# The last two chunks of an attention and mixer kernel: order of ScalarE's copies, step size of the weight sums, and the last pair's banks

## The chip, the cores and the metric

One core of a Trainium2 chip runs the whole program. The metric is the device time of one execution in microseconds. Before the change three runs took 777.46, 777.44 and 774.66 us, median 777.44.

## The reference

The first half is an attention over 32 memory slots per head: weights `a` are a softmax of `phi` over the sequence, they pool keys and values (`k_m`, `v_m`), and each query attends to the pooled keys. Its output, as `x` of 8 x 576 rows and 512 channels, goes through a mixer:

```python
xt = x.transpose(0, 2, 1)
h = np.maximum(xt @ w_tok1, 0.0) @ w_tok2
u = x + h.transpose(0, 2, 1)
h2 = np.maximum(u @ w_ch1, 0.0) @ w_ch2
return (u + h2).astype(np.float32)
```

The change lies in `u + relu(u @ w_ch1) @ w_ch2`, with 1536 hidden channels, for the last 1024 of the 4608 rows.

## The kernel before, in words

All products are made from pairs of parts: a number is split into a high part of fewer bits and the rest (`hh` and `hl`, `c2h` and `c2l` and so on), and three matmuls (high by high, high by low, low by high) stand for one product. The 4608 rows are cut into nine chunks of 512. Chunks 0 to 6 are of no interest here but for their end. Chunks 7 and 8 are of class `Sevens` (L325): there the products with `w_ch1` and with `w_ch2` are both done by a scheme of seven products of half blocks in place of eight (names 11, 22, T1, T3, T2, 21, T4), so that sums and differences of blocks have to be made on VectorE, and split again.

One call of `seven(c, p)` (L2163) handles the pair `p` of hidden blocks, of six, in chunk `c`. TensorE makes the seven first products (six matmuls of 256 columns each) of this pair, with weights in small units that `load_unit` (L539) brings from DRAM, three units ahead. In between, as filling, `mix` hands out the 42 matmuls of the second products of the pair before (`seconds`, L364), which add into seven PSUM banks `m11` to `mT4` (`open_banks`, L339); `shares` says how many come at each of four steps. In the first call, (7,0), the filling is what is left of chunk 6.

The first products use one bank only, `one`, with two halves `a` and `b`. So each step is: two products, a copy of the bank by ScalarE (L2255, L2267, L2281, and of one half L2295), the filling, and then what VectorE and ScalarE make of the copies: adds of the results `r11`, `r12`, `c22`, their ReLU (L2239), the differences T1 to T4, and the split of each into a high part (ScalarE, L124 and L2232) and a low part (VectorE, L127 and L2236). The next products may not write the bank before it is copied. The product T4 of a call is left over to the beginning of the next one.

Every engine takes its instructions in the order of the program text. Besides the pair's own work, `events_at` puts work from other places into the steps, from a table of due times (L1955 to L2059); a call has times `24c + 4p` to that plus 3.5, so (7,0) is 168 to 171.5. Among these are the inputs of chunk 8 (`high`, `low` and the four differences at L276 to L287) and `Tops` (L418): for each of the six pairs of `w_ch2` blocks it makes the sums that the second products need: `words` (high plus low part, 1024 columns, L426), `sum` (four of 256 columns, L465), `high` (L474), `low` (L478). The four due times of a pair are half a unit apart, and the pairs start at 157, 160, 163, 173, 166 and 177. Their results go to rooms that other tiles have left; pairs 0 to 3 have rooms that let one instruction split all four sums, pairs 4 and 5 take four each.

When the last second products of a chunk are done (chunk 7's in (8,0), chunk 8's in (8,5)), `drain` (L379) adds the banks into the output tile `u`: eleven VectorE adds of 512 columns and one ScalarE copy, at the end of the step in which each bank is complete. The last pair of chunk 8 is not done by seven products: its first products give `hid`, the hidden values themselves, and after all of the filling the end (L2333 to L2341) multiplies them with `w_ch2` into five fresh banks, adds each to `u` (L200) and stores it.

Of the kernel before, what the change touches and what calls it, by code (L numbers as in the profile page):

```python
# [20 lines left out]
P = 128  # L21
# [7 lines left out]
def kernel(  # L29
# [295 lines left out]
    class Sevens(Quarters):  # L325
# [38 lines left out]
        def seconds(s, p):  # L364

            for name in ("11", "22", "T1", "T3", "T2", "21", "T4"):
                lh, ll = s.left(name, p)
                h, l = s.right(name)
                for a in range(2):
                    for x, (l_, r) in enumerate(((lh, h), (lh, l), (ll, h))):  # L370
                        first, last = not (a or x or p), a == 1 and x == 2
                        yield 1, name if last else None, lambda name=name, a=a, l_=l_, r=r, first=first: (
                            nc.tensor.matmul(  # L373
                                s.banks[name][:, a], l_[:, a * P : a * P + P], r,
                                start=first, stop=False, skip_group_check=True,
                            )
                        )

        def drain(s, name):  # L379
            V, m = f32(s.rooms2["V"]), s.banks  # L380

            def add(to, x):
                o = s.quarter(int(to[0]) - 1, int(to[1]) - 1) if to != "V" else V
                nc.vector.tensor_tensor(out=o, in0=x, in1=o, op=ALU.add)

            if name == "11":
                nc.scalar.copy(out=V, in_=m["11"])
                add("11", m["11"])
            elif name == "22":
                add("12", m["22"])  # L390
            elif name == "T1":
                add("12", m["T1"])
                add("22", m["T1"])
            elif name == "T2":
                add("V", m["T2"])
                add("12", V)
                add("V", m["T3"])
                add("21", V)
                add("22", V)
            elif name == "21":  # L400
                add("11", m["21"])
            elif name == "T4":
                add("21", m["T4"])

# [13 lines left out]
    class Tops:  # L418
# [5 lines left out]
        def words(s):  # L424
            s.w = sb.tile([P, 2, DM], F32, tag="big", name=f"cw{s.p}", bufs=1)
            nc.vector.tensor_tensor(out=s.w, in0=f32(c2h[s.p]), in1=f32(c2l[s.p]), op=ALU.add)  # L426

        def rooms(s):
            def quad(pool, tag):
                return pool.tile([P, 4, HW], F32R, tag=tag, name=f"top{tag}", bufs=1)  # L430

            if s.p in (0, 3):
                tag = ("kv", "rest")[s.p // 3]
                t = sb.tile([P, 2, 4, HW], F32R, tag=tag, name=f"top{tag}", bufs=1)
                s.merged = [(t[:, 0], t[:, 1])]
            elif s.p < 3:
                s.merged = [tuple(quad(wp, f"w{s.p}{x}") for x in "hl")]
            elif s.p == 4:
# [12 lines left out]
            if s.merged:  # L451
                ((h, l),) = s.merged
                s.pieces = [(h[:, o], l[:, o]) for o in range(4)]
            Sevens.tops[s.p] = dict(zip(("T2", "T3", "22", "T1"), s.pieces))

        def sum(s):
            s.rooms()
            a11, a21, a12, a22 = s.w4 = [s.w[:, j, HW * i : HW * i + HW] for j in range(2) for i in range(2)]
            for to, x, y, op in (
# [4 lines left out]
            ):  # L464
                nc.vector.tensor_tensor(out=to, in0=x, in1=y, op=op)  # L465

        def parts(s):
            if s.merged:
                return [(*s.merged[0], s.w.rearrange("p j (i n) -> p (j i) n", i=2))]
            return [(h, l, w) for (h, l), w in zip(s.pieces, s.w4)]  # L470

        def high(s):
            for h, l, w in s.parts():
                nc.scalar.copy(out=h, in_=w)  # L474

        def low(s):
            for h, l, w in s.parts():
                nc.vector.tensor_tensor(out=l, in0=w, in1=f32(h), op=ALU.subtract)  # L478

# [58 lines left out]

    def load_unit(n):  # L539
        if n >= 2 * NF * (CHUNKS - WIN):  # L540
# [4 lines left out]
        m = 512 if j == 3 else 1024  # L545
        nc.scalar.dma_start(out=f32(t)[:, :m], in_=sums[p].to[:, j, :m])

# [1506 lines left out]
    for n in range(AHEAD):  # L2054
        at(2 * NF * WIN - 4 + n, load_unit, n, k=1)
    for p, h in enumerate((157, 160, 163, 173, 166, 177)):
        top = Tops(p)
        for x, fn in enumerate((top.words, top.sum, top.high, top.low)):
            at(h + x / 2, fn, k=1)  # L2059

# [99 lines left out]

    one, left = [], []

    def seven(c, p):  # L2163
# [9 lines left out]
        T = {**Sevens.T, "T4": C[:, 3]}  # L2173
        todo, final, done, unit = [], None, [], []
        if begin:
            for x, f in before:
                for a in range(NKK):
                    def fn(x=x, f=f, a=a):
                        x.ch2(f, [a])
                        if f == x.end - 1:  # L2180
                            x.add(a)
                    todo.append((6, None, fn))
        else:
            x, f = before
            if not ch.banks:
                ch.open_banks()
            todo += x.seconds(f)
            final = x if f == x.end // 2 - 1 else None
        shares = (12, 12, 12, 12) if begin else (10, 10, 9, 6, 7) if end else (12, 11, 11, 8)

        def mix(x):
            n = shares[x] if x < len(shares) else 0
            while n > 0 and todo:
                cost, name, fn = todo.pop(0)
                fn()
                n -= cost
                if name and final:
                    done.append(name)

        def drains():  # L2200
            for name in done:
                final.drain(name)
            done.clear()
# [74 lines left out]
        events_at(1, 1.5)  # L2278
        product(5, "22", b, False)
        product(2, "T2", a, False)  # L2280
        nc.scalar.copy(out=st3, in_=X)  # L2281
        mix(2)
        add(r12, st3[:, 0], st3[:, 1])
        if end:
            relu_high(eh[:, t1], r12)
            relu_low(eh[:, t1], el[:, t1], r12)
        else:
            relu(r12)
            sub(T["T1"], r12, r11)
            T_high("T1")  # L2290
            T_low("T1")
        drains()
        events_at(2, 2.5)
        product(4, "T3", a, False)
        nc.scalar.copy(out=c22, in_=a)  # L2295
        mix(3)
        add(c22, c22, st2[:, 1])
        if end:
            relu_high(oh[:, t1], c22)
            relu_low(oh[:, t1], ol[:, t1], c22)  # L2300
        else:
            high("22", c22)
            sub(T["T3"], c22, r12, True)
            T_high("T3")
            low("22", c22)
            add(T["T2"], T["T3"], r11)
            T_high("T2")
            T_low("T3")
            T_low("T2")
        drains()  # L2310
        events_at(3, 3.5)

        def rest():
            ch.first(a, units[n + 3][:, 0], "T4", False)
            load_unit(n + 3 + AHEAD + 1)

        if end:
            rest()
            mix(4)
            relu_high(oh[:, t0], a)  # L2320
            relu_low(oh[:, t0], ol[:, t0], a)
            drains()
        else:
            left.append(rest)
        assert not todo, todo
        return ch, p
# [99 lines left out]
```

## Time and profile before

| what | us |
|---|---|
| median of three runs | 777.44 |
| lowest and highest | 774.66, 777.46 |
| the profiled execution | 779.87 |
| its span | 778.1 |
| TensorE, matmul busy | 752.4 |
| VectorE busy | 526.1 |
| ScalarE busy | 377.6 |

The span is what the hardware profiler saw of one execution; the 1.8 us beside it lie around it. Busy time is not a limit by itself: a stage is bound by whatever the last of its waits is for. Engines are PE (matmuls on TensorE), PEld (its weight loads), DVE (VectorE), ACT (ScalarE), SP (SyncE). PEclk is the granted TensorE clock as a share of 2.4 GHz. The profile writes tile names without their numbers: `whole` is the tile that holds the copies of the first and the fourth step, `rst` those of the second and third, `m` and `mT` the seven banks, `cw` the sums of weights, `top...` the rooms for their splits, `unit` the first weights, `end` the banks of the last pair.

### The profile page before, as it was taken

How to read it: one execution, taken by the hardware profiler on the slowest of the kernel's cores; microseconds unless marked ns; L12 is line 12 of the kernel's file. 1: busy time of each engine (PE TensorE's matmuls, PEld its weight loads, DVE VectorE, ACT ScalarE, POOL GpSimd, SP SyncE). 2: the span in 40 equal slices, each digit the busy share in tenths (PEclk: the TensorE clock that was granted, in tenths of full speed). 3: DMA queues.
4: the chain of work that ended last, by engine and by line, in shares of the span. 5: the costliest groups of instructions: out<-in, count | busy, mean ns of one | idle time of the engine just before them, and what ended most of it. 6: DMA issues, size and time to landing. Idle time of an engine off the chain costs nothing.

```text
span 778.1 us, 13954 instructions
## 1 busy us (share of the span) xinstructions
PE 752.4 (97%) x5369; PEld 663.7 (85%) x5369; DVE 526.1 (68%) x1025; ACT 377.6 (49%) x841; POOL 83.5 (11%) x79
## 2 busy tenths in 40 slices
PE   9999999999999999999999999999999997998996
PEld 8787888888877888898988898989899887997996
DVE  4989863788486758655865486748555876677566
ACT  5899772333233335453635353536353544563561
POOL 2204323011220230000000000000010000000000
PEclk9999999999999999999999999999999998999999
DMA  9955623574618249694869386847574563554651
GB/s 367 381 207 169 216 92 96 143 258 129 217 32 281 50 156 290 198 299 133 273 202 274 117 255 231 238 158 206 195 206 113 171 200 112 162 164 152 212 166 54
DMA packets 90449, 147.38 MB, mean 189 GB/s; under 512 B 41488, under 2 KB 60304, under 8 KB 86160
## 3 DMA queue, kind: packets, MB, share of 16 engines
q1 hardware_dynamic: 68032, 79.63, 31.4%
q10 hardware_dynamic: 22352, 66.87, 27.7%
q8 instruction: 42, 0.69, 0.4%
q14 instruction: 23, 0.19, 0.1%
HBM read 121.57 MB, written 24.90 MB: 188 GB/s over the span
## 4 chain that ended last, share of the span: by engine, by line
PE 75%; DVE 12%; DMA 5%; ACT 4%; issue 2%; POOL 1%; SPq 0%; ACTq 0%; DVEq 0%; POOLq 0%
PE acc L182 24%; PE cp L159 9%; PE qa L320 8%; PE u L904 7%; PE one L416 6%; PE qb L320 6%; PE Ap L864 2%; PE mT L373 2%; PE m L373 2%; PE sp L720 1%; DMA kv<-in_kv_dram 1%; PE Rp L883 1%; DMA kb<-keys 1%; PE sp L621 1%; DMA unit<-sums 1%
## 5 line engine op out<-in xcount | busy, mean ns | idle before, releaser
L182 PE MATMUL acc<-qhh,c 128*128 128x512 f32 x256 | 99.4, 395 | 0.0
L182 PE MATMUL acc<-hh,c 128*128 128x512 f32 x288 | 96.7, 395 | 0.0
L320 PEld LDWEIGHTS qa<-xT,unit 128*128 128x128 f32 x432 | 61.1, 188 | 6.6 <-ACT whole L2105 0.5
L320 PEld LDWEIGHTS qb<-x,unit 128*128 128x128 f32 x432 | 61.2, 188 | 6.3
L182 PEld LDWEIGHTS acc<-hh,c 128*128 128x128 f32 x288 | 54.1, 188 | 14.4 <-issue 3.1
L320 PE MATMUL qa<-xT,unit 128*128 128x256 f32 x432 | 63.0, 281 | 0.1
L320 PE MATMUL qb<-x,unit 128*128 128x256 f32 x432 | 62.9, 281 | 0.0
L182 PE MATMUL acc<-hl,c 128*128 128x512 f32 x144 | 56.2, 390 | 0.0
L182 PEld LDWEIGHTS acc<-qhh,c 128*128 128x128 f32 x256 | 48.2, 188 | 9.1 <-issue 3.3
L182 PE MATMUL acc<-qal,c 128*128 128x512 f32 x192 | 54.6, 394 | 0.0
L2108 DVE TENSOR_TENSOR whole<-whole 128x256 f32<-128x256 f32 x48 | 20.7, 431 | 45.9 <-ACT whole L2105 45.9
L182 PE MATMUL acc<-qhl,c 128*128 128x512 f32 x128 | 50.9, 398 | 0.7 <-DVE qhl L127 0.7
L159 PE MATMUL cp<-uh,c1h 128*128 128x512 f32 x144 | 51.5, 398 | 0.0
L159 PE MATMUL cp<-ul,c1h 128*128 128x512 f32 x144 | 50.3, 390 | 0.0
L159 PE MATMUL cp<-uh,c1l 128*128 128x512 f32 x144 | 50.3, 390 | 0.0
L2105 ACT COPY whole<-qa 128x256 f32<-128x256 f32 x72 | 26.7, 371 | 47.8 <-PE qa L320 44.9
L127 DVE SCALAR_TENSOR_TENSOR hl<-cp,hh 128x512 fp32r<-128x512 f32 x36 | 24.7, 686 | 34.3 <-ACT hh L124 34.2
L416 PE MATMUL one<-x,unit 128*128 128x256 f32 x288 | 43.9, 298 | 1.7 <-ACT whole L2255 1.5
L416 PEld LDWEIGHTS one<-x,unit 128*128 128x128 f32 x288 | 40.0, 205 | 3.0 <-ACT whole L2255 2.1
L416 PE MATMUL one<-xT,unit 128*128 128x256 f32 x216 | 34.4, 297 | 7.9 <-ACT whole L2295 7.6
L416 PEld LDWEIGHTS one<-xT,unit 128*128 128x128 f32 x216 | 29.5, 198 | 10.0 <-ACT whole L2295 8.9
L2105 ACT COPY whole<-qb 128x256 f32<-128x256 f32 x48 | 17.7, 369 | 35.6 <-PE qb L320 35.5
(337 smaller groups left out, 1809.4 us busy)
## 6 DMA issues: line engine op xcount, KB each, us to landing
unit<-sums ACTq DMA_DIRECT2D x108, 512.0 KB, 3.9
kv<-in_kv_dram SPq DMA_DIRECT2D x12, 1280.0 KB, 8.3
rawc<-in_w_ch_dram SPq DMA_DIRECT2D x12, 1024.0 KB, 7.0
q<-in_q_dram SPq DMA_DIRECT2D x16, 576.0 KB, 6.0
unit<-sums ACTq DMA_DIRECT2D x36, 256.0 KB, 3.3
sums<-sums SPq DMA_DIRECT2D x12, 512.0 KB, 5.9
phi<-in_phi_dram SPq DMA_DIRECT2D x16, 320.0 KB, 5.5
out_dram<-u SPq DMA_DIRECT2D x5, 1024.0 KB, 5.0
```

The costliest lines, as they stand in the source:

```text
L127: nc.vector.scalar_tensor_tensor(out=l, in0=ps, scalar=0.0, in1=f32(h), op0=ALU.max, op1=ALU.subtract)
L159: nc.tensor.matmul(ps, l[:, a, w], r[:, a], start=n == 0, stop=n == len(mm) - 1)
L182: nc.tensor.matmul(ps, l_[f // 2][:, f % 2, a * P : (a + 1) * P], r[:, w], start=f == start and x == 0, stop=f == end - 1 and x == 2,)
L320: nc.tensor.matmul(ps[:, :HW], l, r, start=first and n == 0, stop=n == len(mm) - 1, skip_group_check=not first,)
L373: nc.tensor.matmul(s.banks[name][:, a], l_[:, a * P : a * P + P], r, start=first, stop=False, skip_group_check=True,)
L416: nc.tensor.matmul(ps, l, r, start=start and n == 0, stop=False, skip_group_check=True)
L621: nc.tensor.matmul(s.kvp[32 * i : 32 * i + 32, : 2 * D], s.pt[:, i, j, :], s.kv[:, :, j, i, :], start=j == 0, stop=j == NC - 1,)
L720: nc.tensor.matmul(s.sp[hf][m, :HALF], s.kb[w, m], s.qT[w, i], start=True, stop=True)
L864: nc.tensor.matmul(ps[:, :TT], a, w, start=x == 0, stop=x == len(mm) - 1)
L904: nc.tensor.matmul(ps[:, :HALF], a, r, start=x == 0, stop=x == len(mm) - 1)
L2105: nc.scalar.copy(out=to, in_=ps[:, :HW])
L2108: nc.vector.tensor_tensor(out=to, in0=x, in1=y, op=ALU.add)
```

## The change

1. Splits move. The differences T1, T3 and T2 are still made in the last step of a call, but their splits and that of `c22` now come in the next call: 22, T1 and T3 behind the copy of its first step, T2 behind the second, together with 21 and T4. The add of `r11` stays in the second step, its ReLU and split go to the third, behind the copy there; the add of `r12` stays in the third, its ReLU goes to the fourth.
2. The filling becomes one list, `stream`, that runs on over the calls, with shares 11, 11, 11, 9; in (7,1) they are 6, 11, 11, 8, so that six matmuls more are always left over from there on.
3. The adds of the banks become single entries of a list, `drains`, of which each step takes two or three, into the following call if need be.
4. `load_unit` in these calls issues from SP and no longer from ScalarE's queue.
5. `Tops` becomes one sequence of small steps, half a unit of time apart: `words` in two halves, four sums, then the copies, then the differences; splits of the whole become two of half the size. Pair 3 now takes rooms with four splits, pair 5 those with two. They start at 156, 161, 166, 171, 178 and 185.
6. The last pair: in place of fresh banks for 128 channels by 512 rows, the last pair's products go straight on top of three of the seven banks (22, 21 and T4), each the quarter that the bank belongs to, and of one free bank, with 12 matmuls of 256 columns each; the order is by which half of `hid` is ready first. These three banks are no longer drained by themselves.

The core of the diff:

```diff
+                return lambda: nc.vector.tensor_tensor(out=o, in0=x, in1=o, op=ALU.add)
+
+            return {
+                "11": [lambda: nc.scalar.copy(out=V, in_=m["11"]), add("11", m["11"])],
+                "22": [add("12", m["22"])],
+                "T1": [add("12", m["T1"]), add("22", m["T1"])],
+                "T3": [],
+                "T2": [add("V", m["T2"]), add("12", V), add("V", m["T3"]), add("22", V), add("21", V)],
+                "21": [add("11", m["21"])],
+                "T4": [add("21", m["T4"])],
+            }[name]
+
+        def direct(s, i, t, fs, ps, start=False):
+
+            for a in range(2):
+                for n, f in enumerate(fs):
+                    h, l = s.hid[f]
+                    for x, (l_, r) in enumerate(((c2h, h), (c2h, l), (c2l, h))):
+                        nc.tensor.matmul(
+                            ps[:, a],
+                            l_[f // 2][:, f % 2, (2 * i + a) * P : (2 * i + a + 1) * P],
+                            r[:, t * HW : (t + 1) * HW],
+                            start=start and not (a or n or x), stop=False, skip_group_check=True,
+                        )
...
-            nc.vector.tensor_tensor(out=s.w, in0=f32(c2h[s.p]), in1=f32(c2l[s.p]), op=ALU.add)
+            for j in range(2):
+                yield lambda j=j: nc.vector.tensor_tensor(
+                    out=s.w[:, j], in0=f32(c2h[s.p][:, j]), in1=f32(c2l[s.p][:, j]), op=ALU.add
+                )
...
+        def steps(s):
+
+            yield from s.words()
             s.rooms()
+            a11, a21, a12, a22 = w = [s.w[:, j, HW * i : HW * i + HW] for j in range(2) for i in range(2)]
             for to, x, y, op in (
                 (a22, a21, a22, ALU.add),
                 (a21, a11, a21, ALU.subtract),
                 (a11, a22, a11, ALU.subtract),
                 (a12, a12, a11, ALU.subtract),
             ):
+                yield lambda to=to, x=x, y=y, op=op: nc.vector.tensor_tensor(out=to, in0=x, in1=y, op=op)
+            parts = [(h, l, x) for (h, l), x in zip(s.pieces, w)]
             if s.merged:
+                parts = [
+                    (h, l, s.w[:, j].rearrange("p (i n) -> p i n", i=2)) for j, (h, l) in enumerate(s.merged)
+                ]
+            for h, l, x in parts:
+                yield lambda h=h, x=x: nc.scalar.copy(out=h, in_=x)
+            for h, l, x in parts:
+                yield lambda h=h, l=l, x=x: nc.vector.tensor_tensor(out=l, in0=x, in1=f32(h), op=ALU.subtract)
...
-    for p, h in enumerate((157, 160, 163, 173, 166, 177)):
-        top = Tops(p)
-        for x, fn in enumerate((top.words, top.sum, top.high, top.low)):
-            at(h + x / 2, fn, k=1)
+    for p, h in enumerate((156, 161, 166, 171, 178, 185)):
+        top = Tops(p).steps()
+        for x in range(14 if p in (3, 4) else 10):
+            at(h + x / 2, lambda top=top: next(top)(), k=1)
...
+            for name, fn in x.seconds(f):
+                stream.append((1, fn))
+                if name and f == x.end // 2 - 1 and not (x is ch and name in ("22", "21", "T4")):
+                    stream.append((0, lambda name=name, x=x: drains.extend(x.drain(name))))
-        shares = (12, 12, 12, 12) if begin else (10, 10, 9, 6, 7) if end else (12, 11, 11, 8)
-
-        def mix(x):
-            n = shares[x] if x < len(shares) else 0
...
-                load_unit(n + k // 2 + AHEAD + 1)
+                load_unit(n + k // 2 + AHEAD + 1, nc.sync)
...
-        mix(0)
+        mix(shares[0])
         if not begin:
+            high("22", c22)
+            T_high("T1")
+            T_high("T3")
+            low("22", c22)
+            T_low("T1")
+            T_low("T3")
             sub(T["T4"], st1[:, 0], T["T2"], True)
-            high("21", st1[:, 0])
-            T_high("T4")
-            low("21", st1[:, 0])
-            T_low("T4")
-        drains()
+        drain(3)
         events_at(0, 0.5)
         product(3, "T1", b, True)
         product(0, "11", a, False)
         nc.scalar.copy(out=st2, in_=X)
-        mix(1)
+        mix(shares[1])
+        if not begin:
+            T_high("T2")
+            high("21", st1[:, 0])
+            T_high("T4")
+            T_low("T2")
+            low("21", st1[:, 0])
+            T_low("T4")
         add(r11, st2[:, 0], st1[:, 1])
+        drain(2)
+        events_at(1, 1.5)
+        product(5, "22", b, False)
+        product(2, "T2", a, False)
+        nc.scalar.copy(out=st3, in_=X)
+        mix(shares[2])
         if end:
             relu_high(eh[:, t0], r11)
             relu_low(eh[:, t0], el[:, t0], r11)
...
             relu(r11)
             high("11", r11)
             low("11", r11)
-        drains()
-        events_at(1, 1.5)
-        product(5, "22", b, False)
-        product(2, "T2", a, False)
-        nc.scalar.copy(out=st3, in_=X)
-        mix(2)
         add(r12, st3[:, 0], st3[:, 1])
+        drain(2)
+        events_at(2, 2.5)
+        product(4, "T3", a, False)
+        nc.scalar.copy(out=c22, in_=a)
+        mix(shares[3])
+        add(c22, c22, st2[:, 1])
         if end:
             relu_high(eh[:, t1], r12)
             relu_low(eh[:, t1], el[:, t1], r12)
+            relu_high(oh[:, t1], c22)
+            relu_low(oh[:, t1], ol[:, t1], c22)
         else:
             relu(r12)
             sub(T["T1"], r12, r11)
-            T_high("T1")
-            T_low("T1")
-        drains()
-        events_at(2, 2.5)
-        product(4, "T3", a, False)
-        nc.scalar.copy(out=c22, in_=a)
-        mix(3)
-        add(c22, c22, st2[:, 1])
-        if end:
-            relu_high(oh[:, t1], c22)
-            relu_low(oh[:, t1], ol[:, t1], c22)
-        else:
-            high("22", c22)
             sub(T["T3"], c22, r12, True)
-            T_high("T3")
-            low("22", c22)
             add(T["T2"], T["T3"], r11)
-            T_high("T2")
-            T_low("T3")
-            T_low("T2")
-        drains()
+        drain(3)
         events_at(3, 3.5)
 
...
-    banks = [(pat, "at", 2)] * 2 + [(pacc, f"acc{a}", 1) for a in range(3)]
-    whole, halves = slice(0, CW), [slice(0, CW // 2), slice(CW // 2, CW)]
-    pieces = [(a, whole) for a in range(NKK - 1)] + [(NKK - 1, w) for w in halves]
-    for x, ((a, w), (pool, tag, n)) in enumerate(zip(pieces, banks)):
-        ps = pool.tile([P, CW], F32, tag=tag, name=f"end{x}", bufs=n)[:, : w.stop - w.start]
-        last.second(ps, a, range(last.end, NF), last.end, NF, w)
-        last.add(a, w, ps)
-        last.store(w, slice(a, a + 1), (nc.scalar, nc.sync)[x % 2])
+    free = pat.tile([P, 2, HW], F32, tag="at", name="free", bufs=2)
+    banks = {"12": last.banks["22"], "22": free, "11": last.banks["21"], "21": last.banks["T4"]}
+    for x, (name, ps) in enumerate(banks.items()):
+        i, t = int(name[0]) - 1, int(name[1]) - 1
+        last.direct(i, t, range(last.end, NF), ps, name == "22")
+        for fn in drains[: 2 - x // 2]:
+            fn()
+        del drains[: 2 - x // 2]
+        for a in range(2) if x == 3 else (slice(0, 2),):
+            o = last.quarter(i, t)[:, a]
+            nc.vector.tensor_tensor(out=o, in0=ps[:, a], in1=o, op=ALU.add)
+            (nc.scalar, nc.sync)[(x + (a == 1)) % 2].dma_start(
+                out=out[last.c, :, 2 * i : 2 * i + 2, t * HW : (t + 1) * HW][:, a], in_=o
+            )
+    assert not drains, drains
```

## Rows read from the trace of the kernel before

**Rows 1.** Page: busy time by engine; DMA issues, us to landing

```profile
PE 752.4 (97%) x5369; PEld 663.7 (85%) x5369; DVE 526.1 (68%) x1025; ACT 377.6 (49%) x841; POOL 83.5 (11%) x79
...
unit<-sums ACTq DMA_DIRECT2D x108, 512.0 KB, 3.9
```

**Rows 2.** Stretches of one call: length, busy us of each engine, clock, DMA

```profile
core 0: us, PE busy (x) PEld busy (x) DVE busy (x) ACT busy (x) POOL busy (x), PEclk, DMA share, GB/s
...
620.15:632.12 11.97, 10.47 (x62) 8.55 (x60) 9.62 (x21) 5.93 (x15) 0.00 (x0) 1.00 0.43 145
632.12:646.49 14.37, 11.13 (x84) 10.31 (x84) 10.34 (x23) 6.65 (x14) 0.00 (x0) 0.98 0.64 211
646.49:663.00 16.51, 13.28 (x84) 12.87 (x85) 11.06 (x25) 7.99 (x19) 0.00 (x0) 0.81 0.36 113
663.00:674.62 11.62, 11.62 (x85) 11.59 (x85) 7.10 (x18) 5.82 (x13) 0.00 (x0) 0.86 0.45 146
684.78:695.74 10.96, 10.58 (x87) 10.18 (x85) 7.58 (x19) 6.82 (x15) 0.00 (x0) 1.00 0.56 167
695.74:708.24 12.50, 10.83 (x85) 10.22 (x85) 10.31 (x24) 7.19 (x16) 0.00 (x0) 1.00 0.49 150
708.24:723.00 14.76, 12.35 (x85) 11.70 (x85) 9.98 (x23) 5.78 (x13) 0.00 (x0) 0.88 0.59 196
...
743.32:753.49 10.17, 10.17 (x87) 10.14 (x85) 5.70 (x16) 5.79 (x13) 0.00 (x0) 1.00 0.61 182
```

**Rows 3.** Waits of PE, 560 to 778.1: total us, times, longest

```profile
PE one L416 <- ACT whole L2295: 7.6, 5, 3.1
PE end L182 <- DVE hid L127: 2.4, 1, 2.4
```

**Rows 4.** Time line around one long wait: start, length, what, idle before

```profile
641.74 1.81 DVE L465 TENSOR_TENSOR cw<-cw 128x256 f32<-128x256 f32 x4
643.91 0.42 ACT L2239 ACTIVATE rst<-rst 128x256 f32<-128x256 f32 x1 [2.40 <-DVE rst L2229]
645.13 1.04 ACT L474 CAST toprest<-cw 128x1024 fp32r<-128x1024 f32 x1
646.08 0.36 ACT L2295 COPY whole<-one 128x256 f32<-128x256 f32 x1
646.49 1.65 PE L416 MATMUL one<-xT,unit 128*128 128x256 f32 x6 [2.61 <-ACT whole L2295]
```

**Rows 5.** Stretches after that wait, columns as in rows 2

```profile
646.50:648.00 1.50, 1.50 (x7) 1.50 (x8) 1.47 (x3) 0.20 (x1) 0.00 (x0) 0.50 0.66 265
653.00:654.00 1.00, 1.00 (x11) 1.00 (x10) 0.00 (x0) 0.20 (x1) 0.00 (x0) 1.00 0.33 131
```

**Rows 6.** Time line of the end of the last call and the tail

```profile
767.65 0.42 DVE L127 SCALAR_TENSOR_TENSOR hid<-one,hid 128x256 fp32r<-128x256 f32 x1
768.12 6.50 PE L182 MATMUL end<-hid,c 128*128 128x512 f32 x26 [2.41 <-DVE hid L127]
774.66 0.42 DVE L200 TENSOR_TENSOR u<-end,u 128x256 f32<-128x256 f32 x1 [0.29 <-PE end L182]
```

**Rows 7.** Time line of a call without excess

```profile
734.04 0.42 DVE L127 SCALAR_TENSOR_TENSOR r<-whole,r 128x256 fp32r<-128x256 f32 x1
734.38 0.42 DVE L2229 TENSOR_TENSOR sT<-sT,rst 128x256 f32<-128x256 f32 x1
735.26 0.59 ACT L2255 COPY whole<-one 128x512 f32<-128x512 f32 x1
736.34 0.41 ACT L2232 CAST rT<-whole 128x256 fp32r<-128x256 f32 x1
736.35 0.33 ACTq L546 DMA_DIRECT2D unit<-sums  x1
```

**Rows 8.** Groups of instructions, 640 to 778.1: busy us, mean ns of one

```profile
L426 DVE TENSOR_TENSOR cw<-c 128x1024 f32<-128x1024 f32 x2 | 2.4, 1218 | 0.0
L384 DVE TENSOR_TENSOR u<-m,u 128x512 f32<-128x512 f32 x6 | 4.0, 685 | 0.1
```

More of the change, by code (lines that the diff above doesn't have):

```diff
@@ L371, in seconds @@
                         first, last = not (a or x or p), a == 1 and x == 2
-                        yield 1, name if last else None, lambda name=name, a=a, l_=l_, r=r, first=first: (
+                        yield name if last else None, lambda name=name, a=a, l_=l_, r=r, first=first: (
                             nc.tensor.matmul(
@@ L383, in add @@
                 o = s.quarter(int(to[0]) - 1, int(to[1]) - 1) if to != "V" else V
[L384 to L403, printed above, removed]
+                return lambda: nc.vector.tensor_tensor(out=o, in0=x, in1=o, op=ALU.add)
[19 more added lines that the diff above has]
+                        )
         def first(s, ps, weights, name, start):
@@ L430, in quad @@
                 return pool.tile([P, 4, HW], F32R, tag=tag, name=f"top{tag}", bufs=1)
-            if s.p in (0, 3):
-                tag = ("kv", "rest")[s.p // 3]
+            if s.p in (0, 5):
+                tag = ("kv", "rest")[s.p // 5]
                 t = sb.tile([P, 2, 4, HW], F32R, tag=tag, name=f"top{tag}", bufs=1)
-                s.merged = [(t[:, 0], t[:, 1])]
+                s.pieces = [(t[:, 0, o], t[:, 1, o]) for o in range(4)]
+                s.merged = [(t[:, 0, o : o + 2], t[:, 1, o : o + 2]) for o in (0, 2)]
             elif s.p < 3:
-                s.merged = [tuple(quad(wp, f"w{s.p}{x}") for x in "hl")]
+                h, l = (quad(wp, f"w{s.p}{x}") for x in "hl")
+                s.pieces = [(h[:, o], l[:, o]) for o in range(4)]
+                s.merged = [(h[:, o : o + 2], l[:, o : o + 2]) for o in (0, 2)]
             elif s.p == 4:
@@ L450, in rooms @@
                     s.pieces.append((t[:, 0], t[:, 1]))
-            if s.merged:
-                ((h, l),) = s.merged
-                s.pieces = [(h[:, o], l[:, o]) for o in range(4)]
             Sevens.tops[s.p] = dict(zip(("T2", "T3", "22", "T1"), s.pieces))
-        def sum(s):
+        def steps(s):
+            yield from s.words()
             s.rooms()
-            a11, a21, a12, a22 = s.w4 = [s.w[:, j, HW * i : HW * i + HW] for j in range(2) for i in range(2)]
+            a11, a21, a12, a22 = w = [s.w[:, j, HW * i : HW * i + HW] for j in range(2) for i in range(2)]
             for to, x, y, op in (
@@ L464, in sum @@
             ):
-                nc.vector.tensor_tensor(out=to, in0=x, in1=y, op=op)
-        def parts(s):
+                yield lambda to=to, x=x, y=y, op=op: nc.vector.tensor_tensor(out=to, in0=x, in1=y, op=op)
+            parts = [(h, l, x) for (h, l), x in zip(s.pieces, w)]
             if s.merged:
[L469 to L478, printed above, removed]
+                parts = [
[5 more added lines that the diff above has]
+                yield lambda h=h, l=l, x=x: nc.vector.tensor_tensor(out=l, in0=x, in1=f32(h), op=ALU.subtract)
     Sevens.tops = {}
@@ L537, with load_unit @@
     units = {}
-    def load_unit(n):
+    def load_unit(n, eng=nc.scalar):
         if n >= 2 * NF * (CHUNKS - WIN):
@@ L545, in load_unit @@
         m = 512 if j == 3 else 1024
-        nc.scalar.dma_start(out=f32(t)[:, :m], in_=sums[p].to[:, j, :m])
+        eng.dma_start(out=f32(t)[:, :m], in_=sums[p].to[:, j, :m])
     sums = []
@@ L2159 @@
             quarters(c, p)
-    one, left = [], []
+    one, left, stream, drains = [], [], [], []
     def seven(c, p):
@@ L2173, in seven @@
         T = {**Sevens.T, "T4": C[:, 3]}
-        todo, final, done, unit = [], None, [], []
         if begin:
@@ L2181, in fn, with mix, drain @@
                             x.add(a)
-                    todo.append((6, None, fn))
+                    stream.append((6, fn))
         else:
-            x, f = before
             if not ch.banks:
                 ch.open_banks()
-            todo += x.seconds(f)
-            final = x if f == x.end // 2 - 1 else None
-        shares = (12, 12, 12, 12) if begin else (10, 10, 9, 6, 7) if end else (12, 11, 11, 8)
-        def mix(x):
-            n = shares[x] if x < len(shares) else 0
-            while n > 0 and todo:
-                cost, name, fn = todo.pop(0)
+            x, f = before
+            for name, fn in x.seconds(f):
+                stream.append((1, fn))
+                if name and f == x.end // 2 - 1 and not (x is ch and name in ("22", "21", "T4")):
+                    stream.append((0, lambda name=name, x=x: drains.extend(x.drain(name))))
+        shares = (12, 12, 12, 12) if begin else (11, 11, 11, 9)
+        if (c, p) == (CHUNKS - 2, 1):
+            shares = (6, 11, 11, 8)
+        def mix(n):
+            while n > 0 and stream:
+                cost, fn = stream.pop(0)
                 fn()
                 n -= cost
[L2197 to L2203, printed above, removed]
+            while stream and not stream[0][0]:
+                stream.pop(0)[1]()
+        def drain(n):
+            for fn in drains[:n]:
+                fn()
+            del drains[:n]
         def product(k, name, to, start):
@@ L2314, in rest @@
             ch.first(a, units[n + 3][:, 0], "T4", False)
-            load_unit(n + 3 + AHEAD + 1)
+            load_unit(n + 3 + AHEAD + 1, nc.sync)
         if end:
             rest()
-            mix(4)
+            mix(99)
             relu_high(oh[:, t0], a)
             relu_low(oh[:, t0], ol[:, t0], a)
-            drains()
+            assert not stream, stream
         else:
             left.append(rest)
-        assert not todo, todo
         return ch, p
```

1 line of the change is left out of this document (added).

## The prediction, made before any run of the changed kernel

> **What bounds the kernel now.** I read the page first. TensorE is busy 97% of the span and no other engine above 68% [rows 1], so a change to the others can pay only where TensorE waits for them or runs slowly. The waits of PE name one stretch alone: from 560 us on they all lie between 620 and 768 us, the calls of `seven` and the tail. The largest group is the first product of a call waiting for ScalarE's copy of line 2295, 7.6 us in five waits; the largest single wait elsewhere is that of the tail, 2.4 us [rows 3].
>
> I call a call by its chunk and its pair, (7,0) to (8,5), and its four parts steps 0 to 3. A call is 84 matmul units of 256 columns (seven products of six, 42 units of the pair before). Undisturbed it takes 10.16 to 10.17 us, or 0.121 us a unit: one of four such calls is shown [rows 2]. What the others take beyond 10.16 is the excess: (7,0) 1.81, (7,1) 4.21, (7,2) 6.35, (7,3) 1.46, (7,5) 0.80, (8,0) 2.34, (8,1) 4.60; in all 21.6 us.
>
> How it arises is seen in the time line [rows 4]. The four sums of a chunk's weights keep VectorE from 641.74 to 643.55; the add of `r12` comes behind them, ScalarE's ReLU waits 2.40 us for it, the 1.04 us copy of the weights follows, and only then, at 646.08, the copy of the one bank. TensorE stood for 2.61 us. Its granted clock is then 0.50, the 1.2 GHz level, for about six microseconds, and 1.00 again at 653 [rows 5]. So a late copy is paid twice; (7,2) holds the slow stretch as well as the next wait.
>
> **The change, part by part.** All costs are against the profiled execution, 779.87 us, of which 778.1 are span; the median of the runs, 777.44, is 2.43 lower, and I take differences over to it unchanged.
>
> (a) *ScalarE's queue.* The splits of a step's results move one step later, so that each bank copy comes ahead of whatever waits for VectorE. In an undisturbed call this is the sequence from the call's start: T4 and 21 end at 1.45; the copy (0.59 [rows 7]) runs from about 1.65 to 2.25, while 11 units fill TensorE to 2.8. The copy has half a microsecond to spare, as it has at the next two steps; line 2295's has 0.4 (0.36 against nine units). Then ScalarE makes three high parts at 0.41 each [rows 7] by 3.5, and VectorE's low part of 22 is there at 3.1; it is first read at 4.3. So the deferred splits are just in time, with 1.2 us to spare.
>
> (b) *Sums of weights in small steps.* The two sums of 1024 columns at 1.22 us become halves at 0.69 [rows 8], and the splits of four chunks become halves: ten VectorE and four ScalarE instructions more. A half pair costs 0.15 us more when nothing overlaps, 1.5 us in all, spread over ten calls; no step has more than two such pieces. In the first three calls VectorE was busy 9.62 + 10.34 + 11.06 = 31.0 us [rows 2]. Counting the pieces, some 11.7 us of weight work leave these calls and 8 come in (halves at 0.6, quarters at 0.34 apart), with 0.6 of a split of chunk 8: about 28 us in 29.8. It fits, tightly.
>
> Independent VectorE instructions of 256 columns start 0.34 us apart though each lasts 0.42 [rows 7]: they overlap by 0.08. The Trainium skill (VectorE: DVE Perf Modes, The DRAIN you can't avoid) says that the next one does not start until the pipe is empty, and advises few instructions, which speaks against small steps. By that, an estimate from 70 instructions in three calls puts 5.6 us more on VectorE there, and the forecast would be about 761. The row here shows the overlap, so I go by the row.
>
> (c) *Adds of the seven banks, two or three a step.* (8,0) and (8,1) had 6.94 us of excess. Eleven adds of 0.69 (0.6 apart) go from one call to two. VectorE has 5.70 us of work in a plain call [rows 2]; (8,0) then has 5.7 + 6 x 0.6 + two splits 1.2 = 10.5, (8,1) 8.7. The excess of (8,0) carries about half a microsecond into (8,1), within the slack of (a).
>
> (d) *Loads from SP.* Four issues a call leave ScalarE's queue. An issue of 0.33 starts with a running cast [rows 7], so I book nothing. On SP they stand behind two stores of a chunk, which wait for its last adds. A load is wanted four units of weights, or some 11 us, later and lands in 3.9 [rows 1], so about 7 us cover a late store. If that cover were gone, each us of lateness would stop TensorE once per store.
>
> (e) *The last pair.* From 753.49, where (8,5) starts, to the last matmul at 774.62 are 21.1 us [rows 2, 6]. The work is 138 units, 16.7 us. The rest is the 2.41 us wait for `hid`, late because VectorE adds T2's and T3's banks ahead of it, and the low clock behind that wait. Afterwards the 48 units of the last pair begin with the quarters whose `hid` is ready first: the half that comes from T4 is read 24 units, 2.9 us, later. By my count VectorE has it at 14.0 from the call's start and TensorE wants it at 14.9. Six units move here from (7,1), at no net cost. The final add and store are of the same size as before. So up to 4.4 us go.
>
> *New waits.* (7,1) has but six units behind its first copy, 0.15 us too few. VectorE's work in (7,0) is 10.8 us (adds 2.4, the take 1.2 as for line 426 [rows 8], weights 3.2, chunk 7's last splits 1.2, its own seven 2.8); the low part of 22 in (7,1) comes behind all of it, at 633.2 to 636.7, and is wanted at 634.2. I bound this wait by 0 and 2.5 us and take 1.5, the middle of the two passes that I made through the queue (1.4 with independent starts overlapped, 2.5 without). In (7,2) and (7,5) a split of chunk 8 on ScalarE still waits for VectorE ahead of a copy: 0.75 and 0.8. (8,1): 0.5. Low clock behind these: 0 (the waits of (7,0) left it at 1.00) to 3.1 (0.19 of the 16.51 us of (7,2)) [rows 2]; I take 0.8, nearer to the first, since the wait is nearer to those of (7,0).
>
> **Sum:** 21.6 + 4.4 = 26.0 recoverable, less 0.15 + 1.5 + 0.75 + 0.8 + 0.5 + 0.8 = 4.5: a gain of 21.5. The execution like the profiled one would take 758.4 and the median 755.9 us.
>
> **Rivals.**
> - *All of the excess goes* (VectorE's queue is never late): 777.44 - 26.0 = 751.4. For it: four calls without any excess in the same loop [rows 2]. Against: the first three calls leave VectorE 6% of room. Chance 0.12.
> - *VectorE becomes the bound of (7,0) to (7,2) and (8,0) to (8,1).* If its waits for ScalarE are exposed (0.49 us each [rows 4], some four a call in five calls, 10 us), about half the gain is left: 763 to 768. For it: 94% planned load. Against: a queue with other work fills such gaps, and before it was busy 70% of these stretches. Chance 0.16.
> - *No change to speak of.* The loads on SP come late behind the stores and the late splits eat the rest; 774 to 781. Against: 7 us of cover. Chance 0.05.
> - *Slower: the deferred splits come late in every call.* The place is the first read of 22's low part in step 1, which today is ready a whole step ahead in plain calls. The slack is 1.2 us. If ScalarE and VectorE got there 2.6 us late in each of ten calls, each would cost that and up to 3.1 of low clock, 57 us against 26 gained: some 808. It breaks even at 2.6 us without the clock, or near 1.5 with it. Against: both engines are busy under 6 us of a plain call's 10.16 [rows 2]. Chance 0.05.
>
> **How the numbers follow.** My forecast has 0.62 (752 to 762). The range 751 to 768 takes in the clean case and most of the bound by VectorE; left out are the last two, the ends of the others and a miscounted term, together under 0.2. A measurement of this kernel tells about 0.5%, 3.9 us, from no change: faster by more than that 0.89, within it 0.05, slower 0.06.
>
> **What would show it.** Calls of 10.2 us from (7,3) on; PE's waits for line 2295's copy gone or under 0.5 us each; one wait in (7,1) for the low part of 22, by VectorE; granted clock 1.00 but for a stretch there at most; VectorE over 9 us in each of (7,0) to (7,2); no wait between the last call's products and the last pair. I am wrong if calls (8,2) to (8,4) exceed 10.2, if a load releases TensorE, or if the tail still waits.

## The result: 752.7 us, and the profile after

| | before | changed |
|---|---|---|
| median us (four runs each) | 777.1 | 752.74 |
| lowest to highest | 774.66 to 777.46 | 751.66 to 753.5 |
| span of the profiled execution | 778.1 | 751.7 |
| (7,0) begins, in it | 620.15 | 618.44 |
| from there to the end | 157.95 | 133.26 |

The ratio is 0.9692, interval 0.9668 to 0.9716. The gain of the medians is 24.4 us where 21.5 were forecast; the time lies in the range of 751 to 768, nearer to its lower end. Of the 26.4 us between the spans, 1.7 lie ahead of (7,0). That stretch varies from profile to profile ((7,0) begins between 616.9 and 622.0 in the fourteen profiles), and not by the change: from the pieces that it moves there up to (7,0) both kernels take the same time to 0.1 us. Differences are therefore read from (7,0) to the end: 24.7 us here.

The page of the changed kernel, its head [rows 1]:

```profile
span 751.7 us, 14077 instructions
PE 740.1 (98%) x5387; PEld 656.9 (87%) x5387; DVE 517.0 (69%) x1032; ACT 370.7 (49%) x845; POOL 84.4 (11%) x79
...
PEclk9999999999999999999999999999999999999999
```

TensorE's clock shows no slice below 9 tenths. The stretches of the calls (7,0) to (7,3), (7,5), (8,0) and (8,1), columns as before [rows 2]:

```profile
core 0: us, PE busy (x) PEld busy (x) DVE busy (x) ACT busy (x) POOL busy (x), PEclk, DMA share, GB/s
618.44:628.28 9.84, 9.84 (x62) 8.81 (x60) 7.58 (x16) 4.33 (x10) 0.00 (x0) 1.00 0.67 235
628.28:638.93 10.65, 9.82 (x80) 9.46 (x78) 9.81 (x26) 5.96 (x16) 0.00 (x0) 1.00 0.75 270
638.93:649.42 10.49, 10.34 (x86) 10.13 (x85) 7.12 (x20) 6.62 (x17) 0.00 (x0) 1.00 0.58 177
649.42:659.50 10.08, 10.08 (x86) 10.08 (x85) 8.89 (x24) 6.29 (x18) 0.00 (x0) 1.00 0.59 184
...
669.58:680.09 10.51, 10.34 (x87) 10.14 (x85) 9.19 (x23) 7.13 (x18) 0.00 (x0) 1.00 0.55 167
680.09:690.17 10.08, 10.08 (x87) 10.08 (x85) 8.49 (x20) 6.59 (x17) 0.00 (x0) 1.00 0.67 224
690.17:700.31 10.14, 10.14 (x87) 10.13 (x85) 10.04 (x23) 4.69 (x12) 0.00 (x0) 1.00 0.59 181
```

The same calls took up to 16.5 us before; plain calls now take 10.08, at granted clock 1.00; what is left over is in (7,1), (7,2) and (7,5), and 0.06 in (8,1). The waits of PE from 612 us on, with total, number and longest, are down to two groups [rows 3]:

```profile
PE m L373 <- DVE r L127: 0.8, 1, 0.8
PE one L420 <- ACT rst L2290: 0.3, 2, 0.2
```

The wait of line 2295's copy, 7.6 us in all before, is gone. The 0.8 is in (7,1), where I had put the largest of the new waits, and for the reason named; VectorE's time line shows it:

```profile
630.06 0.41 DVE L2236 TENSOR_TENSOR whole<-whole,rst 128x256 f32<-128x256 f32 x1
...
631.52 1.28 DVE L431 TENSOR_TENSOR cw<-c 128x512 f32<-128x512 f32 x2
632.72 0.42 DVE L127 SCALAR_TENSOR_TENSOR r<-whole,r 128x256 fp32r<-128x256 f32 x1
```

The two halves of pair 3's first sum (L431) stand ahead of the low part of 22 (632.72); TensorE, which wanted it at 632.2, went on at 633.19. At the end nothing waits any more [rows 6]:

```profile
742.07 1.60 PE L402 MATMUL m<-hid,c 128*128 128x256 f32 x12
...
743.82 0.41 DVE L127 SCALAR_TENSOR_TENSOR hid<-one,hid 128x256 fp32r<-128x256 f32 x1
...
748.03 0.76 DVE L2349 TENSOR_TENSOR u<-mT,u 128x256 f32<-128x256 f32 x2 [0.74 <-PE mT L402]
```

The last pair (`m`, 742.07) follows the seven products at once. The low part that it had waited for before (743.82) is read from 744.95 on. The last two adds begin when TensorE is done and take 0.76 us together, 0.3 more than the single add before.

### The profile page after: what moved, and what is told of

Read it like the earlier page. It is cut to its first block, busy times and chain, and to the rows that moved or that the text cites. A ratio compares the mean times of both kernels' runs of the same rounds, so it can differ in the third digit from the quotient of the medians.

```text
span 751.7 us, 14077 instructions
## 1 busy us (share of the span) xinstructions
PE 740.1 (98%) x5387; PEld 656.9 (87%) x5387; DVE 517.0 (69%) x1032; ACT 370.7 (49%) x845; POOL 84.4 (11%) x79
## 4 chain that ended last, share of the span: by engine, by line
PE 84%; DVE 7%; DMA 3%; issue 3%; ACT 2%; POOL 1%; SPq 0%; DVEq 0%; ACTq 0%; POOLq 0%
PE acc L182 26%; PE cp L159 9%; PE qa L320 9%; PE u L909 8%; PE one L420 7%; PE qb L320 7%; PE mT L373 4%; PE m L373 3%; PE Ap L869 2%; DMA kv<-in_kv_dram 1%; PE sp L725 1%; DMA kb<-keys 1%; PE Rp L888 1%; PE sp L626 1%; PE u L1567 1%
## 5 line engine op out<-in xcount | busy, mean ns | idle before, releaser
L127 DVE SCALAR_TENSOR_TENSOR hl<-cp,hh 128x512 fp32r<-128x512 f32 x36 | 24.7, 687 | 34.7 <-ACT hh L124 34.6
L420 PE MATMUL one<-x,unit 128*128 128x256 f32 x288 | 40.5, 283 | 0.0
L420 PEld LDWEIGHTS one<-x,unit 128*128 128x128 f32 x288 | 37.3, 192 | 0.4 <-ACT whole L2262 0.2
L182 PEld LDWEIGHTS acc<-qal,c 128*128 128x128 f32 x192 | 32.2, 189 | 2.9
L909 PE MATMUL u<-w2h,Rl 128*128 128x288 f32 x112 | 33.0, 295 | 1.1 <-DVE Rl L127 1.1
```

Of the source, the lines that this page charges most:

```text
L127: nc.vector.scalar_tensor_tensor(out=l, in0=ps, scalar=0.0, in1=f32(h), op0=ALU.max, op1=ALU.subtract)
L182: nc.tensor.matmul(ps, l_[f // 2][:, f % 2, a * P : (a + 1) * P], r[:, w], start=f == start and x == 0, stop=f == end - 1 and x == 2,)
L420: nc.tensor.matmul(ps, l, r, start=start and n == 0, stop=False, skip_group_check=True)
L909: nc.tensor.matmul(ps[:, :HALF], a, r, start=x == 0, stop=x == len(mm) - 1)
```

## The experiments

In all of them times are given from the beginning of (7,0) to the end of the span of the profile, beside the median; the changed kernel has 133.26. First each part undone by itself.

**The order of the splits.** The diff moves them back into the step that makes them, for instance

```diff
+        add(r11, st2[:, 0], st1[:, 1])
+        if not end:
+            relu(r11)
+            high("11", r11)
+            low("11", r11)
```

and likewise T1, 22, T3, T2, 21 and T4.

> The changed kernel with one part undone: each split stands again in the step that makes its result, ahead of the next copy of the bank; all else as changed. Theory of the order (the copy of the one bank stood in ScalarE's queue behind work that waits for VectorE, and that made nearly all of the 21.6 us of excess): the calls with weight sums in them get excess back, less than before since the pieces are small; 758 to 765 us, TensorE waiting for the copies of the bank for 3 us or more in all. Rival, theory of the bursts (the 1.8 us and 1.2 us stretches of weight sums on VectorE made it, and in small steps the order is worth nothing): 752.5 to 754 us, waits under 1.5 us in all, as in the changed kernel.

Measured: 149.41 us, median 769.29, above the 758 to 765 expected. (7,1) alone takes 14.51 us in place of 10.65, with a granted clock of 0.88. The waits of PE for two of the copies (total, number, longest):

```profile
PE one L420 <- ACT whole L2262: 6.3, 6, 2.7
PE one L420 <- ACT whole L2299: 4.0, 6, 1.1
```

The time line ahead of the longest, VectorE and ScalarE:

```profile
631.15 1.28 DVE L200 TENSOR_TENSOR u<-acc,u 128x512 f32<-128x512 f32 x2
...
632.35 0.41 DVE L2236 TENSOR_TENSOR whole<-whole,rst 128x256 f32<-128x256 f32 x1
...
632.80 0.42 ACT L124 ACTIVATE r<-whole 128x256 fp32r<-128x256 f32 x1 [3.02 <-DVE whole L2236]
...
634.35 0.58 ACT L2262 COPY whole<-one 128x512 f32<-128x512 f32 x1
```

ScalarE's high part of 22 (632.80) waits 3.02 us for the add at 632.35, which stands behind halves of weights and two adds of chunk 6; the copy of the bank comes behind it at 634.35. The pieces are small and the copy is late all the same. The theory of the order holds, and by more than it had said: 16.2 us above the changed kernel, where 5 to 12 were expected. The theory of the bursts, by which the order is worth nothing in small steps, falls.

**The size of the pieces.** `Tops`, its rooms and its due times as before.

> The changed kernel with the sums of weights as before: four large steps a pair, rooms and due times as before; all else as changed. Theory of the order: the copies no longer stand behind VectorE, so a burst of 4 us on VectorE is felt only where it exceeds the slack of about 1.2 us at the first read of the low part of 22: 753.5 to 757 us, and the waits are for VectorE's low parts, not for the copies. Theory of the bursts: most of the excess of the first three calls comes back, 760 us or more.

Measured: 135.88 us, 2.6 more; median 759.50, above the 753.5 to 757 expected. In the profile another 3.6 lie ahead of (7,0) (622.02), before the first piece that differs; why, no run shows. From (7,0) on the size fits the theory of the order, the place only in part. Of the waits of PE from 612 us on:

```profile
PE one L420 <- ACT whole L2302: 2.0, 2, 1.1
PE acc L182 <- DVE qhl L127: 0.7, 1, 0.7
```

The 0.7 is in (7,0), for a low part of chunk 6 that stands behind a sum on VectorE, as that theory has it. The 2.0 are for a copy. One of the two in the time line:

```profile
640.63 1.80 DVE L469 TENSOR_TENSOR cw<-cw 128x256 f32<-128x256 f32 x4
...
642.47 1.04 ACT L478 CAST toprest<-cw 128x1024 fp32r<-128x1024 f32 x1 [1.29 <-DVE cw L469]
...
643.42 0.36 ACT L2302 COPY whole<-one 128x256 f32<-128x256 f32 x1
```

and TensorE's row behind it:

```profile
643.84 0.98 PE L420 MATMUL one<-xT,unit 128*128 128x256 f32 x6 [1.06 <-ACT whole L2302]
```

Four sums end at 642.4, the 1.04 us cast of the weights waits for them (line 478), and the copy of the bank still stands behind it (line 2302). The new order keeps the pair's own splits out of the copy's way, not the casts from the table of due times; there the small size helps, or another due time (below). Each of those two waits was about 1 us.

**The end.**

```diff
-                if name and f == x.end // 2 - 1 and not (x is ch and name in ("22", "21", "T4")):
+                if name and f == x.end // 2 - 1:
```

and the old lines L2334 to L2341.

> The changed kernel with the end as before: all seven banks are added to the output, the last pair goes into five fresh banks of 512 columns each. Theory: TensorE reaches the last pair at 742.07 of the changed profile and the low part of the last half of the hidden values is ready at about 744.2, so it waits some 2 us, its clock falls for a while after, and the adds of the banks stand ahead of the first store: 755.5 to 758 us. Rival: the six units more at the end already cover the wait, the gain at the end came from the stream: 752.5 to 753.7 us.

Measured: 135.21 us, 1.95 more; median 754.83, between the two expected ranges. The wait is 1.20 us, not 2, and the clock stayed at 1.00. The low part was not earlier than expected: it is ready at 743.17, and (8,5) begins 1.14 us earlier here than in the changed kernel's profile, which makes 744.3 there. VectorE in the time line:

```profile
742.14 0.69 DVE L384 TENSOR_TENSOR u<-rV,u 128x512 f32<-128x512 f32 x1
742.75 0.42 DVE L127 SCALAR_TENSOR_TENSOR hid<-one,hid 128x256 fp32r<-128x256 f32 x1
```

and TensorE's first rows of the end:

```profile
740.93 1.09 PE L182 MATMUL end<-hid,c 128*128 128x512 f32 x4
...
743.22 0.96 PE L182 MATMUL end<-hid,c 128*128 128x512 f32 x3 [1.20 <-DVE hid L127]
```

Four matmuls that do not read it run first, for 1.09 us; the expected 2 us left them out. TensorE's last matmul ends 18.70 us after the beginning of (8,5), 17.44 in the changed kernel; the other 0.7 of the 1.95 us lie behind it, and what makes them is not shown. So of the 3.5 us that the tail gained, the banks bring two; the others come with the rest of the change.

**The adds of the banks.** Each step now empties the list, whatever its length.

> The changed kernel with all adds of a finished bank made in the step in which it is finished, as before, in place of two or three a step. Theory of the order: with the copies first, VectorE may be late by a microsecond in (8,0) without TensorE noticing: 752.3 to 753.7 us. Rival: five adds of 0.6 us in one step exceed the slack and the excess of (8,0) and (8,1) comes back in part: 755 us or more, with waits for VectorE in (8,1).

Measured: 135.47 us, 2.2 more, median 755.13; (8,1) takes 12.0 in place of 10.14. Here my theory was wrong and the rival right. VectorE in the time line of (8,1):

```profile
692.87 0.69 DVE L384 TENSOR_TENSOR rV<-mT,rV 128x512 f32<-128x512 f32 x1
...
695.04 1.29 DVE L384 TENSOR_TENSOR u<-rV,u 128x512 f32<-128x512 f32 x2
...
696.85 0.42 DVE L127 SCALAR_TENSOR_TENSOR r<-whole,r 128x256 fp32r<-128x256 f32 x1
```

and TensorE's row there:

```profile
697.33 0.86 PE L373 MATMUL m<-r,topkv 128*128 128x256 f32 x5 [1.66 <-DVE r L127]
```

Six adds of T2's, T3's and 21's banks run from 692.87 to 696.9, dependent ones 0.72 apart; the low part of 22 (696.85) comes behind them, and TensorE waits 1.66 us. The slack that I worked out for this point was 1.2 us; a burst of 4 us exceeds it.

**The loads.** `load_unit` on ScalarE's queue again.

> The changed kernel with the loads of the weight units issued from ScalarE's queue again. Theory: an issue of 0.33 us runs beside ScalarE's own instruction, and the copies have half a microsecond to spare; 133.0 to 133.6 us from (7,0) on, a median of 752 to 754 us. Rival: an issue stands in front of a copy and takes its slack; waits of TensorE for copies in most calls, 1 us or more in all, 134.3 us or more from (7,0) on.

Measured: 133.27 us, median 753.46, the same three waits. That part of the change does nothing here.

Then two parts alone, on the kernel before. The order here takes in the one list of the filling (part 2 of the change); no run has the list by itself.

> The kernel before with the order alone changed: splits one step later, the filling as one list over the calls; large weight sums, adds of banks at once, loads on ScalarE's queue and the end as before. From the beginning of (7,0) to the end the kernel before takes 157.95 us, the changed one 133.26; undoing the small steps, the late adds and the new end one by one cost 2.6, 2.2 and 1.95. If the parts are independent: about 140.0 us from (7,0) on, a median near 759 us. Rival (the parts cover for one another, so that without them waits add up and the clock falls): 145 us or more from (7,0) on, a median of 764 or more.

Measured: 142.20 us, median 763.05. That lies between the two, 2.2 us above the sum of the parts. The waits of PE from 612 us on show where:

```profile
PE end L182 <- DVE hid L127: 3.0, 1, 3.0
PE one L420 <- ACT whole L2302: 2.0, 2, 1.1
PE m L373 <- DVE r L127: 1.7, 1, 1.7
```

Those for `m` and for line 2302's copies are the ones of the experiments above, with their sizes; but at the end TensorE now waits 3.05 us, with a granted clock of 0.50 behind it (751.5 to 754.5), where the old end alone cost a wait of 1.20. With the adds at once the low part stands behind more of them. These two parts cover for one another. The calls ahead of the end take what they take in the single experiments, to 0.03 us, so the others are independent.

> The kernel before with the weight sums alone in small steps, with their new rooms and due times. Theory of the order: the copies of the bank still stand behind casts that wait for VectorE; 152.5 to 156 us from (7,0) on, a median of 771 to 776 us. Theory of the bursts: the first three calls lose most of their 12.4 us of excess; 148 us or less from (7,0) on, 767 us or less.

Measured: 152.09 us, median 774.65, ratio to the kernel before 0.9992 (0.9971 to 1.0013). The theory of the order had it about right; the theory of the bursts wanted 148 us or less, and (7,1) still takes 13.4 us, (8,1) as long. But the bursts are not without effect. The first three calls take 35.4 us in place of 42.9, so 7.5 of their 12.4 us of excess are gone; some 3 of these are the clock, which stays at 1.00 in (7,2) (0.81 before). (7,3) to (7,5), where pieces now lie, take 3.1 us more.

**What repeats.** That median and that profile differ by more than their noise, so both kernels were profiled a second time.

> The kernel before, profiled a second time. If its excess is made by fixed orders of instructions, 157.5 to 158.4 us from (7,0) on and the same waits at the same places, with (7,0) itself beginning anywhere from 616 to 622 us. Rival: the excess of the first profile was partly that execution's own, 155 us or less.

Measured: 156.49 us, 1.46 less than the first time, below the expected range but above the rival's. All waits from (7,0) on are the same within 0.02 us (2.61 and 3.07 for the longest); (7,2) took 15.31 in place of 16.51, with a granted clock of 0.87 in place of 0.81 [rows 2]:

```profile
645.79:661.10 15.31, 12.07 (x85) 11.67 (x85) 11.07 (x25) 7.96 (x19) 0.00 (x0) 0.87 0.40 125
```

> The kernel before with the weight sums alone in small steps, profiled a second time, since its median of 774.65 stands 1.2 us below that of the kernel before while its profile had 5.9 us less from (7,0) on. If the stretch repeats: 151.8 to 152.4 us from (7,0) on, and the difference lies ahead of it, with (7,0) beginning at 620 or later again. Rival: that profile was a lucky one, 155 us or more.

Measured: 153.56 us, 1.47 more, between the expected range and the rival's, and again with the same waits: (8,1) had the clock at 0.88 in place of 1.00 behind waits of 0.95, 1.86 and 0.47 (0.94, 1.88 and 0.47 in the first). The stretch of (8,1) in the first and in the second execution [rows 2]:

```profile
704.57:717.93 13.36, 10.95 (x85) 10.30 (x85) 9.98 (x23) 5.75 (x13) 0.00 (x0) 1.00 0.58 197
```

```profile
701.99:716.71 14.72, 12.31 (x85) 11.67 (x85) 9.99 (x23) 5.78 (x13) 0.00 (x0) 0.88 0.58 197
```

So the waits are fixed by the order of the instructions, and how long the clock stays low behind one of 2 us is not. With the mean of two profiles, the change brings 157.2 - 133.3 = 24.0 us, which fits the medians. The small steps alone gain 4.4 us in the profiles so averaged and 1.2 in the medians. Most of this lies in which executions were profiled: those of the kernel before took 779.87 and 777.97 us, 2.8 and 1.9 above the medians of 777.1 and 776.04, those of the small steps 774.68 and 774.32, at their median of 774.65. About 1 us stays open.

**A version that is faster in its profiles.** Three due times moved:

```diff
+        if c == CHUNKS - 1:
+            early, late = (0, 0, 1, 2, 4.5), late[:5] + (-2,) + late[6:]
...
-    for p, h in enumerate((156, 161, 166, 171, 178, 185)):
+    for p, h in enumerate((156, 161, 166, 171.5, 178, 185)):
```

> The changed kernel with three due times moved: the weight sums of pair 3 start half a unit later (171.5), so that half of the first sum no longer stands ahead of the low part of 22 in (7,1), and two casts of chunk 8 (T1 and T2) come half a unit later, behind the next copy. Theory (the three waits left, in (7,1), (7,2) and (7,5), are each made by these): up to 1.3 us less, 131.9 to 132.7 us from (7,0) on, call (7,1) below 10.3 and (7,2) and (7,5) at 10.1. Rival: the pieces only move the lateness to the following step; 133.0 us or more from (7,0) on.

Measured: 131.80 us, median 751.69; (7,1) takes 10.06, (7,2) and (7,5) 10.08, and one wait of PE is left:

```profile
PE m L373 <- DVE r L127: 0.2, 1, 0.2
```

So the waits in (7,2) and (7,5) and most of that in (7,1) were made by these three pieces. Beside the changed kernel:

> The changed kernel itself, beside the shifted one and the kernel before. From (7,0) on 133.2 to 133.4 us if that stretch repeats from execution to execution; a median of 752 to 754 us. If it does not repeat within 0.3 us, the differences of 2 us read from single profiles are not to be trusted.

> The changed kernel with the three due times moved. From (7,0) on 131.7 to 131.9 us; its median 1 to 2 us below that of the changed kernel in the same call. Rival: the 1.46 us are given back ahead of (7,0), the medians are equal.

Measured from (7,0) on 133.25 and 131.78, within 0.02 of the first time; medians 752.75 and 751.73, ratios to the kernel before 0.9700 (0.9675 to 0.9726) and 0.9694 (0.9668 to 0.9720). The 1.5 us stand in every profile and the medians are 1.0 apart; the intervals overlap, so as a difference in time it is likely, not shown.

## Why the prediction was right

- *What bounds it:* shown. The copy behind VectorE's work was the cause: undoing the order of the splits alone costs 16.2 us of 24.7, and the order with the one list of the filling, on the kernel before, gives 14.3 to 15.8 of them (by the two profiles of that). The four parts undone one by one cost 16.2, 2.6, 2.2 and 1.95, in all 22.9; what the list brings by itself is not shown.
- *The base:* the 21.6 us of excess were those of one execution. In the second profile the same calls have 20.2, with the same waits and less time at the low clock. So the sum began up to 1.4 us too high, and this offset a part of the new waits that were booked too high (below); that is luck.
- *(a), the slack:* the copies came out as worked out. In call (8,5) of the changed kernel, which begins at 730.55:

```profile
732.19 0.59 ACT L2262 COPY whole<-one 128x512 f32<-128x512 f32 x1 [1.83 <-PE one L420]
...
733.12 0.42 DVE L127 SCALAR_TENSOR_TENSOR r<-whole,r 128x256 fp32r<-128x256 f32 x1 [1.50 <-ACT r L124]
...
733.31 1.60 PE L420 MATMUL one<-x,unit 128*128 128x256 f32 x12
...
734.87 0.40 PE L373 MATMUL m<-r,topqT 128*128 128x256 f32 x2
```

The copy runs from 1.64 to 2.23 and the bank is wanted at 2.76, as forecast to 0.05 us; the low part of 22 is ready at 2.99 and read by the second of the last two matmuls, at 4.44. The slack is some 1.4 us, where 1.2 was forecast. (c) keeps bursts that exceed it away (2.2 us); (b) was worth 2.6, mainly for another reason, the casts ahead of the copy.

- *(b):* the row was right: in the changed kernel two halves run in 1.28 us, where two alone take 0.69 each. The rule of the Trainium skill (VectorE: DVE Perf Modes, The DRAIN you can't avoid), that the next instruction waits until the pipe is empty, stands there with an exception, that an instruction which is not held back starts earlier; the overlap here (1.28 against 1.38) agrees with the exception. By the stretches above VectorE has 24.5 us of work in the first three calls, 7.58, 9.81 and 7.12. I had counted 28, and forecast over 9 in each; this is the step that was mis-sized, and with it the room for new waits. The weight work fell by the 3.7 us counted (12.1 to 8.5 by the lengths of its instructions). Not counted were 1.7 us of other work that now falls outside these calls and 1.0 of more overlap, and the split of chunk 8 (0.6) does not come in.
- *(c):* (8,0) has no excess left and (8,1) 0.06, with 8.49 and 10.04 us of VectorE work, where 10.5 and 8.7 were counted: more of the adds fell into the second call.
- *The new waits:* all four at their places, each smaller than forecast. Above its 78 units (7,1) has 1.3 (1.65 forecast), (7,2) 0.41 (0.75), (7,5) 0.43 (0.80), (8,1) 0.06 (0.50), and the clock did not fall (0.8): 2.2 in place of 4.5.
- *The plain call:* 10.16 was not undisturbed. T4 waited some 0.08 us for the copy in each call; now it is 10.08. Over eleven calls that is 0.9 us that the forecast did not have.
- *(d):* nothing, as booked. *(e):* to the end of TensorE's last matmul 3.7 us (17.44 us from the beginning of (8,5), 21.13 before), as forecast for that place (4.4 less the six units); 0.2 of it is lost again behind that matmul.
- *The rivals:* of the times named, that of the clean case came nearest, and the shifted version all but reaches it. The bound by VectorE showed only where a burst met the first read of a low part: in (7,1) here, in (8,1) with the adds at once, in (7,0) with the large sums. The 0.49 us of that rival stands in no line of [rows 4]; in the plain calls (8,2) to (8,4) before, VectorE's waits for ScalarE last from 0.13 to 1.24 us.

## What to carry to other kernels

When an engine that empties a bank also does work that waits for a third engine, put the copy ahead of all that waits, in the order of its queue, even if the work then is a step late: this was worth 16 us here, and no other part that was undone alone more than 2.6. Then look at what still stands ahead of the copy from elsewhere, and ahead of the first read of what was put off; there a few small pieces matter, and here a due time moved by half a step was enough. Read such changes from a stretch that begins behind the parts that vary.

## What the runs showed that was not expected

The same wait need not be followed by the same clock. Behind waits of 0.95, 1.86 and 0.47 us in (8,1) the granted clock was 1.00 in one execution and 0.88 over the call in another, 1.4 us of time; behind the single 1.20 us wait at the old end it stayed at 1.00, and behind 2.41 at the end of the kernel before it was at 0.50 (769 to 772 us). A wait of this size costs a varying amount, and one execution of such a kernel is uncertain by that much.
